# Token rows kept in order, expert places kept in a table and gathered, mean queries and keys added on GpSimd, and mean-key tiles of 64x128, in a fused attention and mixture-of-experts kernel

## The chip, the cores and the metric

The kernel runs on one core of a Trainium2 chip. The core has five engines, each with its own queue of instructions: TensorE (PE in the rows; its weight loads are listed apart as PEld), VectorE (DVE), ScalarE (ACT), GpSimd (POOL) and SyncE (SP). Transfers run on 16 DMA engines; they are started by SP or by POOL here. The metric is the device time of one execution in microseconds (us); lower is better.

## The reference, cut to what matters

Eight batches of eight heads, 576 positions, head dimension 64. Each head has two attentions: one over the means of four neighbouring positions (144 mean queries against 144 mean keys and values, repeated four times), and one over the seven nearest positions. Their sum, laid out as 4608 tokens of 512 numbers, goes to a top-1 mixture of eight experts.

```python
q_d = q.reshape(B, H, Sd, factor, D).mean(axis=3)      # k_d and v_d likewise; factor = 4, Sd = 144
out_up = np.repeat(sm_attn(q_d, k_d, v_d), factor, axis=2)
mask = np.abs(pos[:, None] - pos[None, :]) < factor
out_local = softmax(where(mask, scale * q @ k.T, -1e9)) @ v
x = (out_up + out_local).transpose(0, 2, 1, 3).reshape(B * S, H * D)
e_idx = np.argmax(x @ w_gate, axis=1)
gate_w = softmax(x @ w_gate)[arange(N), e_idx]
eom = sigmoid(x @ w_output_gate)
for e in range(E):                                     # E = 8
    mask = e_idx == e
    out[mask] = gate_w[mask] * eom[mask, e] * (relu(x[mask] @ w1[e]) @ w2[e])
```

## The kernel before, in words

The work is 32 units, each a pair of heads of one batch; four units make a batch. Three functions put a unit's steps into a plan, and `gate` adds the steps of a batch. `Plan.order` is a list scheduler: each step has an engine, a cost, its inputs and the buffers that it uses, and a priority of ten times its slot plus a number from the table `AT`. It puts the steps of all engines into one order, which then stands fixed in every engine's queue. An engine runs its queue strictly in order, so a step that waits holds up all that stand behind it.

`prep(u)` transposes q and k into `T` (PSUM, two buffers; L382) and, by 16 more matmuls for each of q and k with a quarter of an identity as moving operand (L389, `idq`), adds up the means of four beside the transposes. VectorE copies the transposes out (`qT`, `kT`, L397), ScalarE the means (`qd` L402, `kd` L411). VD takes the mean values (L425), ScalarE copies them into `vd` (L431).

`scores(u)` makes the scores of the mean keys (L447, named DS) and of the band (L460, L470), both into the one buffer `S`, and their exponentials into `e` (L452, L476).

`values(u)` makes mean-key values and denominators (V1, L493: 16 products in 64x64 tiles, four of the array's quarters at a time), band denominators (V2, L503) and band values (V3, L515) into the single buffers `PD` and `PL`; then logarithm, exponential of the negative, products (L523 to L549), and on GpSimd the sum of both attentions `xT` (L556) and its f16 copy `x16` (L559).

`gate(b)` makes the logits (L591, L600), picks the expert, ranks the tokens within their expert (L623 to L629, `cum` carries the counts), turns x16 into token rows `xh` of 516 f16 (512 numbers, coefficient, token number; L670, L674), and scatters each row to its place `pos` in the DRAM table `hx_xs`, which has a region for each expert: six indirect transfers a batch on GpSimd (L679). The first 640 rows of each region are filled beforehand with a row whose token number lies out of range (`prefill`, eight transfers on SP).

After the plan, each expert loads its 640 rows with one transfer on SP (L784), transposes them (L750, L751), and runs up (L759, L762, L764) and down (L769, L771); GpSimd scatters the rows to the output by the token number in the row (L772). An expert with more than 640 tokens would go through a loop behind an `If`. The weights of three experts are loaded during attention (`weights`, L693 and L694, two transfers on GpSimd, with a cast to f16), the others when one of three buffers comes free.

Of the kernel before, what the change touches and what calls it, by code (L numbers as in the profile page):

```python
# [8 lines left out]
F32 = mybir.dt.float32  # L9
# [9 lines left out]
SD = 144  # L19
# [47 lines left out]
class Plan:  # L67
# [3 lines left out]
    NEAR = 0.2  # L71
# [85 lines left out]
def kernel(  # L157
# [19 lines left out]
    XW = Dm + 4  # L177
    REG = N
    scale = 1.0 / (D ** 0.5)

    xs_dram = nc.dram_tensor("hx_xs", (E * REG, XW // 2), I32, kind="Internal")

    cst = ctx.enter_context(tc.tile_pool(name="cst", bufs=1))
    wpool = ctx.enter_context(tc.tile_pool(name="wpool", bufs=3))

# [28 lines left out]
    idq = cst.tile([HB, HB + 16], F16)  # L214
# [4 lines left out]
    on_d = cst.tile([128, 3, 64], F32)  # L219
# [9 lines left out]
    zt = cst.tile([128, XW // 2], I32)  # L229
    kd_s = [cst.tile([128, 3, 128], F16, tag=f"kd{i}", name=f"kd{i}") for i in range(3)]  # L230
# [7 lines left out]
    r_vd = ring(sbA, [128, 3, D], F32, "vd", 2)  # L238
# [9 lines left out]
    r_PD = ring(psA, [128, 2, 512], F32, "PD", 1)  # L248
    r_kd = fixed_ring(kd_s)
# [6 lines left out]
    def c_idq():  # L256
        nc.vector.memset(idq, 0.0)
        nc.vector.tensor_scalar_mul(idq[:, 0:HB], id16[0:HB, 0:HB], 0.25)
        for t in kd_s:
            nc.vector.memset(t, 0.0)  # L260
    t_idq = add("c1", 0, "DVE", 1.0, c_idq, deps=[t_id])
# [30 lines left out]
    def c_pv():  # L292
        nc.vector.memset(pv, 0.0)
        nc.vector.memset(on_l, 1.0)
        nc.vector.memset(on_d, 0.0)
        for g in range(NB):
            n = GI[g + 1] - GI[g]
            if g in (0, 1, 4):
                for h in range(2):
                    r0 = 64 * h + 32 * (g % 2)  # L300
                    on = on_d[r0:r0 + n, g // 2:(g // 2 + 2 if g < 4 else 3), :]
                    nc.vector.memset(on, 1.0)
# [538 lines left out]
```

## Time and profile before

| | us |
|---|---|
| median of 3 runs | 519.19 (516.39 to 520.56) |
| profiled execution, time | 523.01 |
| its span, first to last instruction | 520.9 |
| TensorE busy | 419.6 (81%), 7849 matmuls and as many weight loads |
| VectorE, ScalarE, GpSimd busy | 187.4, 199.2, 177.2 |
[...]

TensorE is the only engine that is busy for more than two fifths of the span. The program has two long stages, attention with the gate (up to about 326 us) and the experts (342.6 to 510.5 us), with different limits; shares over the whole span mix them. TensorE's matmuls are pipelined and overlap, so group times add up to more than the time in which the engine was busy.

### The profile page before, as it was taken

How to read it: one execution, taken by the hardware profiler on the slowest of the kernel's cores; microseconds unless marked ns; L12 is line 12 of the kernel's file. 1: busy time of each engine (PE TensorE's matmuls, PEld its weight loads, DVE VectorE, ACT ScalarE, POOL GpSimd, SP SyncE). 2: the span in 40 equal slices, each digit the busy share in tenths (PEclk: the TensorE clock that was granted, in tenths of full speed). 3: DMA queues.
4: the chain of work that ended last, by engine and by line, in shares of the span. 5: the costliest groups of instructions: out<-in, count | busy, mean ns of one | idle time of the engine just before them, and what ended most of it. 6: DMA issues, size and time to landing. Idle time of an engine off the chain costs nothing.

```text
span 520.9 us, 17550 instructions
## 1 busy us (share of the span) xinstructions
PE 419.6 (81%) x7849; PEld 304.6 (58%) x7849; DVE 187.4 (36%) x496; ACT 199.2 (38%) x449; POOL 177.2 (34%) x211
## 2 busy tenths in 40 slices
PE   3787878978897977987997966089959989999991
PEld 2666757656776765765776754065536646566550
DVE  5232443443463462443463453132213313223220
ACT  2243734553563552433463542023313332333331
POOL 6021522535434534424324453405221340512312
PEclk9986986997787895678697886579989997999997
DMA  8998799382992489272212010227893988873202
GB/s 130 178 194 210 172 213 170 75 124 65 173 170 72 80 135 200 53 119 58 60 43 55 18 34 16 78 69 167 133 259 79 202 165 176 198 158 123 91 24 76
DMA packets 85269, 62.74 MB, mean 120 GB/s; under 512 B 49597, under 2 KB 77245, under 8 KB 85184
## 3 DMA queue, kind: packets, MB, share of 16 engines
q0 software_dynamic: 30624, 40.43, 40.6%
q1 hardware_dynamic: 54560, 21.10, 17.9%
q8 instruction: 63, 1.03, 0.8%
q14 instruction: 22, 0.18, 0.1%
HBM read 68.23 MB, written 20.53 MB: 170 GB/s over the span
## 4 chain that ended last, share of the span: by engine, by line
PE 48%; issue 31%; POOL 8%; DMA 4%; ACT 3%; DVE 2%; another core or an unknown queue 2%; POOLq 1%; SPq 0%; DVEq 0%
PE T L389 9%; PE PD L493 7%; POOL out_dram L772 7%; PE T L382 5%; PE PL L515 5%; PE T L425 4%; PE PD L503 4%; PE T L591 3%; PE T L670 3%; DMA qk<-in_k_dram 2%; PE pu L759 2%; PE S L460 2%; PE S L447 2%; PE py L769 1%
## 5 line engine op out<-in xcount | busy, mean ns | idle before, releaser
L759 PE MATMUL pu<-xgT,w 128*128 128x320 f16 x512 | 75.1, 310 | 1.8 <-DVE xgT L751 1.2
L556 POOL TENSOR_TENSOR xT<-xl,xd 128x576 f32<-128x576 f32 x32 | 38.8, 1212 | 102.1 <-DVE xl L549 101.9
L769 PE MATMUL py<-w,hs 128*128 128x512 f16 x320 | 70.4, 379 | 0.0
L679 POOL DMA_INDIRECT hx_xs<-xh,g_pos x48 | 45.1, 939 | 70.1 <-DVE g_pos L660 24.8
L389 PE MATMUL T<-idq,qk 72*64 72x88 f16 (+1 forms) x1024 | 63.0, 312 | 6.3 <-issue 5.9
L759 PEld LDWEIGHTS <-w 128*128 128x128 f16 x512 | 51.8, 101 | 24.5 <-issue 2.9
L772 POOL DMA_INDIRECT out_dram<-y,xg x40 | 39.2, 979 | 64.0 <-ACT y L771 60.2
L762 ACT ACTIVATE hs<-pu 128x320 f16<-128x320 f32 x64 | 28.0, 437 | 83.3 <-PE pu L759 77.7
L389 PEld LDWEIGHTS <-qk 72*64 72x64 f16 x1024 | 47.5, 166 | 9.2 <-issue 9.2
L769 PEld LDWEIGHTS <-hs 128*128 128x128 f16 x320 | 31.3, 98 | 36.4
L764 DVE TENSOR_SCALAR hs<-pu 128x320 f16<-128x320 f32 x64 | 31.4, 491 | 45.7 <-PE pu L759 37.2
L382 PE MATMUL T<-id,qk 72*64 72x72 f16 x1024 | 35.4, 221 | 14.5 <-DMA qk<-in_q_dram 8.9
L493 PE MATMUL PD<-e,vd 64*64 64x72 f32 (+1 forms) x512 | 42.3, 317 | 5.7 <-issue 3.1
L771 ACT ACTIVATE y<-py,xg 128x512 f32<-128x512 f32 x40 | 27.5, 687 | 47.9 <-PE py L769 47.9
L397 DVE COPY kT<-T 128x576 f16<-128x576 f16 x32 | 24.2, 757 | 56.2 <-ACT kd L411 26.5
L493 PE MATMUL PD<-e,on_d 64*64 64x72 f32 (+1 forms) x512 | 42.2, 318 | 2.6 <-issue 2.6
L751 DVE COPY xgT<-tp 128x1024 f16<-128x1024 f16 (+1 forms) x24 | 13.2, 596 | 84.1 <-PE py L769 42.9
L523 ACT ACTIVATE r<-PD 128x582 f32<-128x582 f32 x32 | 21.0, 656 | 57.5 <-PE PD L503 41.6
L397 DVE COPY qT<-T 128x576 f16<-128x576 f16 x32 | 24.2, 757 | 50.9 <-PE T L389 39.2
L493 PEld LDWEIGHTS PD<-e,vd 64*64 64x64 f32 x512 | 36.2, 173 | 9.4 <-issue 8.6
L382 PEld LDWEIGHTS <-qk 72*64 72x64 f16 x1024 | 28.0, 130 | 23.4 <-issue 9.1
L515 PE MATMUL PL<-e,v 64*64 64x57 f32 (+1 forms) x1280 | 33.1, 252 | 10.0 <-issue 9.1
(109 smaller groups left out, 605.8 us busy)
## 6 DMA issues: line engine op xcount, KB each, us to landing
w<-in_moe_w_dram POOLq DMA_DIRECT2D x16, 1024.0 KB
v<-in_v_dram SPq DMA_DIRECT2D x128, 80.0 KB, 4.8
hx_xs<-zt SPq DMA_DIRECT2D x8, 645.0 KB, 5.8
xg<-hx_xs SPq DMA_DIRECT2D x8, 645.0 KB, 4.2
qk<-in_q_dram POOLq DMA_DIRECT2D x7, 576.0 KB
qk<-in_k_dram POOLq DMA_DIRECT2D x7, 576.0 KB
hx_xs<-xh,g_pos POOLq DMA_INDIRECT x48
out_dram<-y,xg POOLq DMA_INDIRECT x40
```

Of the source, the lines that this page charges most:

```text
L382: nc.tensor.transpose(t16[64 * h:64 * h + 64, HB * c:HB * c + HB], src.tile[:, 2 * hp + h, D * c:D * c + D], id16[0:HB, 0:HB])
L389: nc.tensor.matmul(_ap(o, [o.ap[0], [2, w]]), lhsT=src.tile[:, 2 * hp + h, D * (4 * a + m):D * (4 * a + m) + D], rhs=idq[:, 0:w], start=(a ...
L397: nc.vector.tensor_copy(xT.tile.rearrange("p (n c) -> p n c", c=8), T.tile.bitcast(F16)[:, 0:S].rearrange("p (c n) -> p n c", c=8))
L493: nc.tensor.matmul(p[o:o + 64, h, WC + q0:WC + q0 + c1 - c0], lhsT=w[r, blk, :], rhs=et[r, i, WC + c0:WC + c1], start=(blk == 0), stop=(bl ...
L515: nc.tensor.matmul(p[64 * h:64 * h + 64, par, c0:c1], lhsT=vbuf.tile[r, g, h, :], rhs=et[r, h, c0:c1], start=(g == 0), stop=True, skip_gro ...
L556: nc.gpsimd.tensor_tensor(xT.tile[:, hp, :].rearrange("p (n m) -> p n m", m=4), xl.tile.rearrange("p (n m) -> p n m", m=4), _bc(xd.tile, 4 ...
L679: ins = nc.gpsimd.indirect_dma_start(out=xs_dram.ap(), out_offset=bass.IndirectOffsetOnAxis(ap=pos.tile[:, j:j + 1], axis=0), in_=xh.tile[ ...
L759: nc.tensor.matmul(pu[:, 0:c1 - c0], lhsT=w1sb[:, c, 128 * f:128 * f + 128], rhs=xgT[:, c, c0:c1], start=(c == 0), stop=(c == 3))
L762: nc.scalar.activation(hs[:, f, c0:c1], pu[:, 0:c1 - c0], AF.Relu)
L764: nc.vector.tensor_scalar_max(hs[:, f, c0:c1], pu[:, 0:c1 - c0], 0.0)
L769: nc.tensor.matmul(py, lhsT=hs[:, f, 128 * j:128 * j + 128], rhs=w2sb[:, f, :], start=(f == 0), stop=(f == NG - 1))
L772: ins = nc.gpsimd.indirect_dma_start(out=out_rows, out_offset=bass.IndirectOffsetOnAxis(ap=xgi[:, j, Dm // 2 + 1:Dm // 2 + 2], axis=0), in ...
```

## The change

There are five parts.

- **Means.** L389's matmuls go. After VectorE has copied `qT` and `kT`, GpSimd adds neighbours twice (L410 then L413 for q; L410 then two adds of 64 partitions at L418 for k), into `qd` and `kd`. They are sums, so the exponential's scale is divided by 16.
- **Mean-key scores** in four matmuls of 128x128 instead of eight of 128x64. `kd` holds both heads in a block-diagonal form either way.
- **Mean-key values and denominators** in six matmuls with 64x128 tiles instead of sixteen with 64x64. `vd` has columns of ones on both sides of the values, so that one matmul makes both.
- **Token rows.** `xh` (514 f16 now) is written in token order by one plain transfer of SP a batch; two of its three copies out of PSUM go to ScalarE. The prefill goes. The place of each token is turned into one-hot rows (`hi`, `lo`), six matmuls (INV) turn them into a table of 128 lanes x 40 columns, `acc`, that holds the token of each place, and at the end `acc` gives the index lists `gidx` and `sidx`.
- **Experts.** GpSimd gathers the rows of an expert by `gidx` with five indirect transfers (L774), two experts ahead and with three buffers; the next expert's transposes stand between the steps of down; the weights of expert e+3 are asked for behind the five scatters of expert e.

The numbers of `AT`, some of the scheduler's costs and NEAR change as well.

```diff
-    "v": -31.38, "Tq": -3.33, "Tk": 1.99, "evq": -4.73, "evk": 4.65, "qd": -21.49, "kd": -8.83, "VD": 15.17,
+    "v": -55.23, "Tq": -9.85, "Tk": 9.68, "evq": -2.54, "evk": -2.5, "qd": 33.27, "kd": -12.34, "VD": 10.97,
...
-                w = HB + 16 * i
-                for a in range(2):
-                    for m in range(4):
-                        for h in range(2):
-                            o = t32[64 * h:64 * h + 64, 2 * SD + a:2 * SD + a + 1]
-                            nc.tensor.matmul(_ap(o, [o.ap[0], [2, w]]),
-                                             lhsT=src.tile[:, 2 * hp + h, D * (4 * a + m):D * (4 * a + m) + D],
-                                             rhs=idq[:, 0:w], start=(a == 0 and m == 0), stop=(m == 3),
-                                             skip_group_check=True)
...
+            def fn(xT=xT, s2=s2, sd=sd, i=i):
+                pairs = xT.tile.rearrange("p (n m) -> p n m", m=2)
+                nc.gpsimd.tensor_tensor(s2.tile[:, 0:S // 2], pairs[:, :, 0], pairs[:, :, 1], op=ALU.add)
+                if i == 0:
+                    pairs = s2.tile.rearrange("p (n m) -> p n m", m=2)
+                    nc.gpsimd.tensor_tensor(sd.tile, pairs[:, :, 0], pairs[:, :, 1], op=ALU.add)
+                else:
+                    for h in range(2):
...
+                        nc.gpsimd.tensor_tensor(o.rearrange("p b (s x) -> p b s x", s=2),
...
+            e2 = add("kd" if i else "qd", n, "POOL", 1.4 if i else 0.9, fn, deps=[ev, t_ks], uses=[xT, s2, sd])
...
+                nc.tensor.matmul(s[:, i, WC + c0:WC + c1], lhsT=kd.tile[:, blk, :], rhs=qd.tile[:, q0:q0 + c1 - c0],
+                                 start=(blk < 2), stop=True, skip_group_check=True)
...
+                    o, x = p[:, h, WC:WC + SD], et[r, blk % 2, WC:WC + SD]
+                    if blk == 2:
+                        o, x = o.rearrange("p (i n) -> p i n", i=2), et[r, :, WC + SD:WC + DC]
+                    nc.tensor.matmul(o, lhsT=vd.tile[r, blk, D - D * h:3 * D - D * h], rhs=x, start=(blk == 0),
+                                     stop=(blk == 2), skip_group_check=True)
...
+        def fn():
+            for j in range(NJ):
+                nc.tensor.matmul(G.tile[:, 0:NC], lhsT=olo.tile[:, j, :], rhs=hit.tile[:, j, :], start=(j == 0),
+                                 stop=(j == NJ - 1), skip_group_check=True)
+        t10 = add("INV", n, "PE", 0.36, fn, deps=[t8, t9], uses=[olo, hit, G], mode=128, lat=0.16)
...
-        for j in range(NJ):
-            def fn(j=j):
-                ins = nc.gpsimd.indirect_dma_start(
-                    out=xs_dram.ap(), out_offset=bass.IndirectOffsetOnAxis(ap=pos.tile[:, j:j + 1], axis=0),
-                    in_=xh.tile[:, j, :].bitcast(I32), in_offset=None, bounds_check=E * REG - 1, oob_is_err=False)
...
+            nc.sync.dma_start(xs_dram.ap()[S * b:S * b + S, :].rearrange("(j p) d -> p j d", p=P),
+                              xh.tile.bitcast(I32))
+        add("put", n, "SP", 0.8, fn, deps=[t6] + rows, uses=[xh], lat=2.5)
...
-    for r in range(E):
-        add("pre", 2 * r + 1, "SP", 0.8, lambda r=r: prefill(r), deps=[t_cg])
...
+        for e in range(E):
+            w1sb, w2sb = wts[e]
+            xgT, hs, y = xts[e]
+            if e + 2 < E:
+                fetch(e + 2)
+            up(xgT, hs, CAPJ, w1sb)
+            if e + 1 < E:
+                xts[e + 1] = tiles(CAPJ)
+            for j in range(CAPJ):
+                col = CAPJ * (E - 1 - e) + j
+                down(xgs[e], hs, y, j, w2sb, sidx[:, col:col + 1], True)
+                if e + 1 < E and 2 * j < CAPJ:
+                    turn(xgs[e + 1], xts[e + 1][0], CAPJ, 2 * j)
+            if e + 3 < E:
+                weights(e + 3)
```

In TensorE's queue, V1 and V2 of one unit in the middle of attention stand like this before: L389 is the last of the k means, L493 V1, L503 V2, L425 VD and L515 V3.

```order
L389 MATMUL T<-idq,qk_679 64x88
L493 MATMUL PD<-e,vd 64x144 x2
L493 MATMUL PD<-e,on_d 64x144 x2
L493 MATMUL PD<-e,vd 64x72 x2
L493 MATMUL PD<-e,on_d 64x72 x2
L503 MATMUL PD<-e,on_l 64x291 x4
L425 MATMUL T<-v,pv 32x64 x12
L515 MATMUL PL<-e,v 64x60 x4
```

In the changed kernel the same steps are L503 (V1), L512 (V2), L524 (V3), L433 (VD) and L455 (mean-key scores), and L396 is the last transpose of a k.

```order
L396 MATMUL T<-id_70,qk_416 64x72
L524 MATMUL PL<-e,v 64x60 x4
L524 MATMUL PL<-e,v 64x57 x12
L433 MATMUL T<-v,pv 32x64 x12
L503 MATMUL PD<-e,vd_95 128x144 x6
L512 MATMUL PD<-e,on_l 64x291 x4
L455 MATMUL S<-qd,kd_98 128x144
L455 MATMUL S<-qd,kd_98 128x72
```

The means are gone from between transposes and values, V1 is one row of six, and over the whole queue the mean-key scores of a unit stand behind the transposes of the unit after it.

In GpSimd's queue of before, in the middle of attention, the sums and copies of the tokens (L556, L559) stand between the scatters (L679) and the loads of q and k (L345).

```order
L556 TENSOR_TENSOR xT<-xl,xd 128x576
L559 CAST x_1550<-xT 128x576
L679 DMA hx_xs<-xh_90,g_pos 36864x258 x4
L556 TENSOR_TENSOR xT<-xl,xd 128x576
L559 CAST x_1550<-xT 128x576
L679 DMA hx_xs<-xh_90,g_pos 36864x258 x2
L345 DMA qk_2356<-in_q_dram 72x8x512
```

In the changed kernel the same place has the adds for q (L410, L413) and k (L410, L418) of later units between the token sums (L565) and copies (L568).

```order
L410 TENSOR_TENSOR ks_99<-kT 128x288
L418 TENSOR_TENSOR kd_98<-ks_99 64x3x64 x2
L410 TENSOR_TENSOR qs<-qT 128x288
L413 TENSOR_TENSOR qd<-qs 128x144
L565 TENSOR_TENSOR xT<-xl,xd 128x576
L410 TENSOR_TENSOR ks_100<-kT 128x288
L418 TENSOR_TENSOR kd_96<-ks_100 64x3x64 x2
L568 CAST x_4713<-xT 128x576
```

The scatters have left the queue, and five adds a unit have come in, in one line with the steps that wait for VectorE's products.

In the expert stage GpSimd's queue has scatters of the output (L772) and weight loads (L693, L694) before.

```order
L693 DMA w_7638<-in_moe_w_dram 128x4x1024
L772 DMA out_dram<-y,xg 4608x512 x4
L694 DMA w_7639<-in_moe_w_dram 128x8x512
L772 DMA out_dram<-y,xg 4608x512
L693 DMA w_7834<-in_moe_w_dram 128x4x1024
```

In the changed kernel the gathers (L774) come first for three experts, and then once an expert, behind the scatters (L807) and the weights (L726, L727).

```order
L774 DMA xg<-hx_xs,gidx 128x257 x15
L807 DMA out_dram<-y,sidx 4608x512 x5
L726 DMA w_5957<-in_moe_w_dram 128x4x1024
L727 DMA w_5958<-in_moe_w_dram 128x8x512
L774 DMA xg<-hx_xs,gidx 128x257 x5
```

The row loads have moved from SP's queue, where nothing stands behind them but each other, to GpSimd's, behind two weight transfers.

## Rows read from the trace of the kernel before

**Rows 1.** Windows: stages; engine busy (instructions), granted clock, DMA share, GB/s.

```profile
26.20:307.60 281.40, 235.83 (x6415) 188.84 (x6412) 125.20 (x336) 135.00 (x324) 106.48 (x116) 0.81 0.59 114
...
342.60:510.50 167.90, 155.37 (x972) 92.99 (x971) 43.29 (x86) 54.77 (x103) 46.71 (x49) 0.95 0.64 141
```

**Rows 2.** Groups of TensorE from 26.2 to 307.6 us (first and last of 16).

```profile
L389 PE MATMUL T<-idq,qk 72*64 72x72 f16 (+1 forms) x928 | 55.4, 303 | 6.3 <-issue 5.9
...
L629 PE MATMUL T<-cum,ones 96*96 96x48 f16 x7 | 1.5, 210 | 0.0
```

**Rows 3.** Waits of TensorE in the same window: first and eleventh of its reasons.

```profile
PE T L425 <- issue: 11.9, 18, 2.4
...
PE T L591 <- issue: 0.6, 2, 0.4
```

**Rows 4.** Timeline, last unit of attention.

```profile
309.95 0.92 POOL L679 DMA_INDIRECT hx_xs<-xh,g_pos  x1 [0.30 <-issue]
...
311.81 0.35 PE L515 MATMUL PL<-e,v 64*64 64x57 f32 x5 [1.01 <-issue]
...
314.68 0.68 PE L515 MATMUL PL<-e,v 64*64 64x57 f32 x11 [0.47 <-issue]
314.71 0.66 ACT L523 ACTIVATE r<-PD 128x582 f32<-128x582 f32 x1 [9.14 <-remote]
```

**Rows 5.** Windows: the 12 spells of scatters before the last, summed up.

```profile
sum 55.20, PE 36.67 PEld 22.65 DVE 18.00 ACT 9.28 POOL 46.71; mean PE 3.06 PEld 1.89 DVE 1.50 ACT 0.77 POOL 3.89
```

**Rows 6.** Windows of 3 us around one spell of scatters.

```profile
162.00:165.00 3.00, 1.44 (x26) 0.82 (x27) 0.00 (x0) 0.66 (x1) 2.67 (x3) 0.80 0.32 92
165.00:168.00 3.00, 3.00 (x91) 2.72 (x85) 1.06 (x3) 2.07 (x6) 0.70 (x2) 0.50 0.03 5
...
174.00:177.00 3.00, 3.00 (x123) 2.66 (x117) 1.21 (x2) 2.04 (x4) 0.26 (x1) 0.99 0.14 33
```

**Rows 7.** Timeline: V1 and what follows, at full and at half clock.

```profile
301.95 0.34 PE L493 MATMUL PD<-e,vd 64*64 64x144 f32 x2
302.75 0.67 PE L503 MATMUL PD<-e,on_l 64*64 64x291 f32 x8
...
287.90 0.51 PE L493 MATMUL PD<-e,vd 64*64 64x144 f32 x2
289.39 1.02 PE L503 MATMUL PD<-e,on_l 64*64 64x291 f32 x8
290.24 0.75 PE L515 MATMUL PL<-e,v 64*64 64x60 f32 x40
290.92 0.65 PE L670 MATMUL T<-id,x 128*96 128x128 f16 x8
```

**Rows 8.** Groups of GpSimd from 26.2 to 307.6 us.

```profile
L556 POOL TENSOR_TENSOR xT<-xl,xd 128x576 f32<-128x576 f32 x30 | 36.3, 1211 | 98.8 <-DVE xl L549 98.6
L679 POOL DMA_INDIRECT hx_xs<-xh,g_pos x38 | 35.9, 944 | 61.3 <-DVE g_pos L660 24.8 <-DVE xh L674 19.1 <-DMA v<-in_v_dram 8.6
```

**Rows 9.** Chain of waits: start, us, what.

```profile
332.73 2.37 DMA hx_xs<-xh,g_pos
335.69 4.18 DMA xg<-hx_xs
```

**Rows 10.** Timeline, expert stage.

```profile
352.34 8.80 PE L769 MATMUL py<-w,hs 128*128 128x512 f16 x40
...
360.97 1.06 PE L750 MATMUL tp<-id,xg 128*128 128x128 f16 x16
...
362.37 0.38 PE L750 MATMUL tp<-id,xg 128*128 128x128 f16 x4 [0.34 <-DVE xgT L751]
...
362.96 8.85 PE L759 MATMUL pu<-xgT,w 128*128 128x320 f16 x64 [0.21 <-issue]
...
371.65 3.62 PE L769 MATMUL py<-w,hs 128*128 128x512 f16 x16
...
386.62 2.40 PE L750 MATMUL tp<-id,xg 128*128 128x128 f16 x20 [6.17 <-DMA xg<-hx_xs]
```

More of the change, by code (lines that the diff above doesn't have):

```diff
@@ new lines, with count, gather @@
+    more = cst.tile([128, E], I32)
+    most = cst.tile([128, 1], I32)
+    def count():
+        nc.vector.tensor_scalar(more, cntf, scalar1=127.0 - 128.0 * CAPJ, scalar2=0.0, op0=ALU.add, op1=ALU.max)
+        nc.vector.tensor_scalar(more, more, scalar1=7, scalar2=None, op0=ALU.arith_shift_right)
+        nc.vector.tensor_reduce(most, more, axis=AX.X, op=ALU.max)
+    def gather(xg, nj, idx, c0):
+        for j in range(nj):
+            nc.gpsimd.indirect_dma_start(
+                out=xg[:, j, :], out_offset=None, in_=xs_dram.ap(),
+                in_offset=bass.IndirectOffsetOnAxis(ap=idx[:, c0 + j:c0 + j + 1], axis=0),
+                bounds_check=N - 1, oob_is_err=False)
@@ L755, in experts, with turn, up @@
+    def turn(xg, xgT, nj, j0):
+        w = min(2, nj - j0)
+        tp = psF.tile([128, 2, 4, 128], F16, tag="T", name="T", bufs=2)
+        x16 = xg.bitcast(F16)
+        for j in range(w):
+            for c in range(4):
+                nc.tensor.transpose(tp[:, j, c, :], x16[:, j0 + j, 128 * c:128 * c + 128], id16)
+        nc.vector.tensor_copy(xgT.rearrange("p c (j n) -> p j c n", n=128)[:, j0:j0 + w], tp[:, 0:w])
+    def up(xgT, hs, nj, w1sb):
         for f in range(NG):
[L756 to L757 removed]
+            for i in range(2):
+                c0, c1 = 64 * nj * i, 64 * nj * (i + 1)
+                pu = psF.tile([128, 512], F32, tag="U", name="U", bufs=4)
@@ L779, with down @@
-    for e in range(E):
-        if e not in wts:
-            weights(e)
-        base = (E - 1 - e) * REG
-        xg = sbF.tile([128, CAPJ, XW // 2], I32, tag="xg")
-        nc.sync.dma_start(xg, xs_dram.ap()[base:base + 128 * CAPJ, :].rearrange("(j p) d -> p j d", p=128))
-        experts(xg, CAPJ, *wts[e], True)
+    def down(xg, hs, y, j, w2sb, idx, group):
+        py = psF.tile([128, Dm], F32, tag="Y", name="Y", bufs=2)
+        for f in range(NG):
+            nc.tensor.matmul(py, lhsT=hs[:, f, 128 * j:128 * j + 128], rhs=w2sb[:, f, :],
+                             start=(f == 0), stop=(f == NG - 1))
+        nc.scalar.activation(y[:, j, :], py, AF.Copy, scale=xg[:, j, Dm // 2:XW // 2].bitcast(F32))
+        ins = nc.gpsimd.indirect_dma_start(
+            out=out, out_offset=bass.IndirectOffsetOnAxis(ap=idx, axis=0),
+            in_=y[:, j, :], in_offset=None, bounds_check=N - 1, oob_is_err=False)
+        if group:
+            tc.declare_no_dep(ins.ins, group="out_scatter", reason="the rows differ")
+            tc.add_to_no_dep_group("out_scatter", ins.ins)
@@ new lines, in tiles, with fetch @@
+    def tiles(nj):
+        return (sbF.tile([128, 4, 128 * nj], F16, tag="xgT", name="xgT"),
+                sbF.tile([128, NG, 128 * nj], F16, tag="hs", name="hs"),
+                sbF.tile([128, nj, Dm], F32, tag="y", name="y"))
+    with tc.manual_schedule():
+        xgs, xts = {}, {}
+        def fetch(e):
+            xgs[e] = gpool.tile([128, CAPJ, XW // 2], I32, tag="xg", name="xg")
+            gather(xgs[e], CAPJ, gidx, CAPJ * (E - 1 - e))
+        fetch(0)
+        fetch(1)
+        count()
+        xts[0] = tiles(CAPJ)
+        for j0 in range(0, CAPJ, 2):
+            turn(xgs[0], xts[0][0], CAPJ, j0)
+        for e in range(E):
[13 more added lines that the diff above has]
+                weights(e + 3)
@@ L792 @@
         posi = cst.tile([128, 1], I32)
+        ids = cst.tile([128, 1], I32)
+        tok = cst.tile([TB, 1], I32)
+        for b in range(B):
+            for j in range(NJ):
+                nc.vector.tensor_scalar(tok, tok_i[0:TB, j:j + 1], scalar1=float(S * b), scalar2=None, op0=ALU.add)
+                nc.vector.tensor_scalar(posi[0:TB], posall[:, b, j:j + 1], scalar1=float(-REG), scalar2=None, op0=ALU.add)
+                nc.gpsimd.indirect_dma_start(
+                    out=id_dram.ap(), out_offset=bass.IndirectOffsetOnAxis(ap=posi[0:TB], axis=0),
+                    in_=tok, in_offset=None, bounds_check=E * REG - 1, oob_is_err=False)
         for e in range(E):
```

214 lines of the change are left out of this document (100 added, 114 removed), and 12 rows, old and new, of the table AT.

## The prediction

> **What bounds the kernel now.** I read the page's shares first and then left them: TensorE is busy for 81% of the span, but attention and the experts have different limits. So the next view was windows by stage [rows 1]. From the first V1 (26.2 us) to the last (307.6) lie 31 units in 281.4 us, 9.08 us a unit. TensorE is busy for 235.8 of them, 7.61 a unit; VectorE 4.04, ScalarE 4.35, GpSimd 3.43. TensorE sets the pace, with 45.6 us of idle time, 1.47 a unit. Its groups show what it does [rows 2], its waits what stops it [rows 3]: ten of the 14 reasons read "issue", in all 38.7 us, from the first with 11.9 down to 0.2. Real waits for another engine come to under 4 us.
>
> Where the issue stalls fall is to be seen in the timeline [rows 4]: while GpSimd issues scatters one after another, TensorE gets five matmuls, then nothing for a microsecond, and ScalarE sits for 9.14 us. The 12 spells of scatters in the 281 us, taken together [rows 5], hold 55.2 - 36.7 = 18.5 us of TensorE's idle time, 41% of it in 20% of the time. [...]
>
> In the experts (167.9 us for eight, 21.0 each) TensorE is busy for 155.4. Up takes 8.69 us from its start to the start of down, down 8.63, the transposes 1.06 + 0.38 [rows 10]; together 18.8. The rest is waits for rows like the 6.17 us there, a slow clock behind them, and copies between transposes and up.
>
> **The sum is made against the profiled execution**, 523.0 us; its span is 520.9. The median of the runs, 519.2, is 0.7% lower, and I scale by that at the end.
>
> **Means off TensorE.** The 16 groups of [rows 2], L389 first and L629 last, add up to 284.5 us with V1's two simultaneous halves counted once; TensorE was busy for 235.8, so a group's us count 0.83. L389's 55.4 are then 45.9, 1.48 a unit. The end above is 1.79 (no overlap); below I take 1.1. It lies on the path, since TensorE is what the others wait for.
>
> **V1 and the mean-key scores.** 32 matmuls in the trace become 12 and 8 become 4, but columns stay: before, four quarters ran at once over 144 + 144 + 72 + 72 columns, now two halves run over three times 144. So V1, 0.80 us at full clock and 1.49 at half [rows 7], need not shrink: between nothing and a quarter of it, 0.3 a unit; I take 0.1 for both steps, since at half clock it takes 1.86 times as long, as work does that follows the columns. V1 now has another tile shape than V2 behind it. Between V2 and V3, of one shape, starts overlap the end before by 0.17 us, between V3 and a transpose of another shape by 0.07 [rows 7]: 0.1 a change, one or two more a unit. [...] The table's six matmuls a batch (INV), at some 0.2 us start to end, cost 0.08 a unit at most. Busy per unit: 7.61 - 1.48 - 0.1 + 0.1 + 0.1 = 6.2; I use 6.1.
>
> **Scatters out of attention.** The 0.60 us a unit of idle time in the spells goes; one transfer of SP takes the place of six issues on GpSimd and stands on SP only before loads of v that have some units to spare. The issue stalls left, 1.25 - 0.60, shrink with the instructions, of which TensorE fetches a quarter fewer in this stage (1024 + 640 + 128 matmuls go of some 6860, with their loads): 0.49. The 0.22 of other waits stay. Idle: 0.71, pace 6.8. The clock, 0.81 of full now, should gain: five of the spells are followed by such a stretch at half clock, nine us worth about 3.7 each, 0.6 a unit; half of it, 0.3, I take back, since other idle time may pull it down as well. For new waits I add 0.2. **Pace 6.7**, 31 x 2.38 = 74 us saved.
>
> **What the adds cost GpSimd.** 3.43 us a unit less the scatters' 35.9 / 31 leaves 2.27 [rows 1, 8]. The only two-input add of the trace makes 576 elements in 1211 ns, 2.1 ns each. The new ones make 288 + 144 and 288 + 192 + 192 elements: 2.3 us by elements; at the price of the whole row for each of the five, 6.1. So GpSimd has 4.6 to 8.3 us a unit. I take the lower end and some, 5.0, since the adds are half or a third of the row's size; then it is below the pace. They also read f16 with a step of two, which no row shows. [...] The delay itself is covered: mean-key scores stand behind the transposes of the next unit, a slack of about one unit, 6.7 us, against VectorE's copy and at most 3.3 us of adds. If that cover fails, TensorE waits, and V1, V2 and V3 with it.
>
> VectorE loses two of three row copies and gains the one-hots, a few tenths a unit; ScalarE loses the copies of means, gains those two. Both stay below 4.6. The prologue has more constants on VectorE ahead of its first copy, but waits for q and k as before; nothing, plus or minus 3 us.
>
> **The hand-over** from the last V1 to the first up (35 us). V3 of the last unit, 5.3 us among the scatters, needs about 1.3 without them: 4. Then, before, six scatters at 1.22 from 326.6, their landing by 335.1 and the load by 339.9 [rows 4, 9]: 13.3. Now some 3 us of table (VectorE, six matmuls, VectorE), five gathers at 1.22, 2.4 to land: 11.5, with transposes beside the gathers: 3 less with that. Saved: 7, between 2 and 10.
>
> **The experts.** 8 x 18.8 less the first transposes is 148.7, plus 1.0 for a first up at half clock: 149.7 instead of 167.9. The transposes inside down hide their copies; row loads no longer wait for scatters. Saved: 18.
>
> **Sum:** 74 + 7 + 18 = 99; 523 - 99 = 424, scaled to the median 421.
>
> **The rivals.** *GpSimd sets the pace* (0.12): at the price of the full row 8.3 us a unit, saving 24 instead of 74: 470. For it: the queue is strict, adds stand behind token sums that wait for VectorE (98.6 us now [rows 8]). Against it: the two-input add's price should go with its size.
>
> *Half clock* (0.12): with less work TensorE idles more between short steps, and the clock stays at 0.50. V1 takes 1.49 us there against 0.80 [rows 7]; over all steps I take 1.7. The clock of 0.81 means 38% of the time at half, so 6.1 is 5.1 at full and 8.7 at half clock; with 0.3 idle 9.0, no gain in pace: 519 - 2 - 7 - 18 = 492. Against it: the low stretches follow the spells that go.
>
> *Late rows in the experts* (0.10): gathers stand behind two weight transfers, and DMA is at 0.64 over the stage already [rows 1]. Five experts late by some 4 us: 441. For it the waits of before; against it, each gather has about 1.4 experts' time.
>
> *Slower* (0.03): the adds again, but dearer than any row, by their steps of two. From 1.5 us an add GpSimd needs 9.9 a unit, which eats all the rest; at 1.8 the time is 519 + 31 x 2.2 - 25 = 562. That the change does not do what it says is no case: the queues show it.
>
> **How the numbers follow.** The forecast has 0.63. At full clock throughout and 0.9 idle the pace is 6.0, and 519 - 95 - 25 gives 399; I go to 396. Upward the range takes in late rows (441) and most of GpSimd's pace up to 8.2, 468. Half clock, the end of the GpSimd case and slower, some 0.2, lie outside. A measurement of this kernel can tell about 1% from no change. Faster by more than that: 0.95; slower: 0.03; within: 0.02.
>
> **What would show it.** First V1 to last V1 in 200 to 215 us; TensorE busy 6.1 a unit there; no stalls of a microsecond every five matmuls; adds of 0.6, 0.3 and 0.4 us; clock over 0.85 in attention; 18.8 us an expert without waits for xg. The prediction is wrong if the mean-key scores wait for GpSimd in most units, or if the issue stalls stay although the scatters are gone.

## The result, and the profile after

The changed kernel takes 440.16 us (median, 438.84 to 442.69) against 519.88 us (one execution more than in the table of the kernel before): a ratio of 0.847, 95% interval 0.840 to 0.853. Each ratio in this document is taken over the undisturbed executions of both kernels alone, so it need not be that of the medians. The profiled execution took 438.8 us with a span of 437.0 and a mean granted TensorE clock of 0.902; that of the kernel before had 0.851. Its page, with the busy times, the granted clock by slices and the chain of waits by engine:

```profile
PE 347.9 (80%) x6105; PEld 244.9 (56%) x6105; DVE 222.0 (51%) x550; ACT 180.7 (41%) x369; POOL 261.4 (60%) x363
...
PEclk9998997686977889989999855889999999999996
...
PE 39%; DVE 16%; POOL 16%; issue 12%; DMA 8%; ACT 5%; POOLq 1%; DVEq 0%; ACTq 0%
```

In the page of the kernel before, the chain was this:

```profile
PE 48%; issue 31%; POOL 8%; DMA 4%; ACT 3%; DVE 2%; another core or an unknown queue 2%; POOLq 1%; SPq 0%; DVEq 0%
```

"Issue" has fallen from 31% to 12% of the chain, VectorE and GpSimd have come up to 16% each. That fall is not TensorE's stalls in the main: of the 160 us of issue in the chain before, 114 lie in the experts, where the chain runs along GpSimd's scatters. TensorE's own waits are shown below. The windows by stage (attention from the first V1 to the last; the hand-over; the experts) answer to [rows 1]:

```profile
23.10:244.60 221.50, 178.44 (x4845) 140.33 (x4842) 152.88 (x359) 119.30 (x253) 154.17 (x229) 0.89 0.68 123
244.60:271.10 26.50, 12.55 (x145) 9.01 (x146) 12.01 (x44) 4.61 (x9) 10.87 (x11) 0.59 0.25 69
271.10:426.60 155.50, 151.19 (x974) 90.78 (x972) 44.36 (x86) 54.70 (x104) 81.22 (x82) 0.97 0.65 155
```

A unit takes 221.5 / 31 = 7.15 us instead of 9.08: busy 5.76, idle 1.39. Of the 83.9 us that the span lost, 59.9 are here, 8.5 in the hand-over (35.0 to 26.5), 12.4 from the first up to the end and 3.1 ahead of the first V1. TensorE's waits in attention (us in total, times, longest) are of another kind than [rows 3]:

```profile
PE S L468 <- ACT e L460: 9.5, 5, 2.2
PE S L455 <- POOL kd L418: 5.7, 10, 1.0
PE T L706 <- DVE qT L402: 5.4, 6, 1.2
PE PD L503 <- DVE xd L547: 4.3, 5, 1.2
PE T L433 <- issue: 3.2, 2, 2.4
```

Summed over all rows of that view, issue has gone from 38.7 to 10.0 us, and waits for the other three engines from 6.2 (with the last V1's own) to 32.2. In the expert stage nothing waits for rows, and a whole expert takes 18.4 us, except the first: its up starts at 271.1 and down only at 288.0, 16.9 us where each later expert takes 8.7 and the sum had 9.7 for the first, in pieces as in [rows 4]:

```profile
275.60 3.23 PE L794 MATMUL U<-xgT,w 128*128 128x320 f16 x19
280.25 0.70 PE L794 MATMUL U<-xgT,w 128*128 128x320 f16 x4 [1.43 <-issue]
282.32 0.70 PE L794 MATMUL U<-xgT,w 128*128 128x320 f16 x4 [1.37 <-ACT hs L797]
```

Beside it GpSimd issues the ten gathers of the next two experts, one every 1.30 us.

### The profile page after: what moved, and what is told of

Same layout as the page of the kernel before. It is cut to its first block, busy times and chain, and to the rows that moved or that the text cites. A ratio compares the mean times of both kernels' runs of the same rounds, so it can differ in the third digit from the quotient of the medians.

```text
span 437.0 us, 14182 instructions
## 1 busy us (share of the span) xinstructions
PE 347.9 (80%) x6105; PEld 244.9 (56%) x6105; DVE 222.0 (51%) x550; ACT 180.7 (41%) x369; POOL 261.4 (60%) x363
## 4 chain that ended last, share of the span: by engine, by line
PE 39%; DVE 16%; POOL 16%; issue 12%; DMA 8%; ACT 5%; POOLq 1%; DVEq 0%; ACTq 0%
PE U L794 12%; PE Y L804 10%; PE PD L503 4%; POOL xT L565 3%; DMA w<-in_moe_w_dram 3%; DMA qk<-in_k_dram 3%; PE PD L512 3%; POOL out_dram L807 3%; DVE kT L402 2%; DVE xl L554 2%; PE T L706 2%; POOL kd L418 2%; DVE xd L547 2%; ACT r L540 2%; DVE g_og L644 2%
## 5 line engine op out<-in xcount | busy, mean ns | idle before, releaser
L807 POOL DMA_INDIRECT out_dram<-y,sidx x40 | 39.7, 993 | 64.8 <-ACT y L806 35.0
L794 PE MATMUL U<-xgT,w 128*128 128x320 f16 x512 | 75.5, 310 | 3.6 <-issue 1.4
L804 PE MATMUL Y<-w,hs 128*128 128x512 f16 x320 | 73.8, 379 | 0.0
L799 DVE TENSOR_SCALAR hs<-U 128x320 f16<-128x320 f32 x64 | 31.4, 492 | 68.5 <-PE U L794 57.2
L565 POOL TENSOR_TENSOR xT<-xl,xd 128x576 f32<-128x576 f32 x32 | 38.7, 1210 | 24.8 <-DVE xl L558 24.2
L774 POOL DMA_INDIRECT xg<-hx_xs,gidx x40 | 40.7, 1018 | 21.3 <-issue 11.3
L797 ACT ACTIVATE hs<-U 128x320 f16<-128x320 f32 x64 | 27.9, 437 | 59.2 <-PE U L794 58.0
L806 ACT ACTIVATE y<-Y,xg 128x512 f32<-128x512 f32 x40 | 27.5, 688 | 55.7 <-PE Y L804 38.0
L804 PEld LDWEIGHTS <-hs 128*128 128x128 f16 x320 | 30.5, 98 | 31.5
L503 PE MATMUL PD<-e,vd 64*128 64x144 f32 x384 | 40.6, 352 | 5.3 <-DVE xd L547 4.3
L396 PE MATMUL T<-id,qk 72*64 72x72 f16 x1024 | 28.8, 214 | 19.3 <-DMA qk<-in_q_dram 14.0
L410 POOL TENSOR_TENSOR ks<-kT 128x288 f32<-128x288 f16 x32 | 21.9, 685 | 28.9 <-DVE kT L402 28.7
L396 PEld LDWEIGHTS <-qk 72*64 72x64 f16 x1024 | 23.8, 124 | 26.6 <-DMA qk<-in_q_dram 14.2
L503 PEld LDWEIGHTS PD<-e,vd 64*128 64x128 f32 x384 | 32.7, 230 | 7.8 <-issue 2.8
L418 POOL TENSOR_TENSOR kd<-ks 64x192 f16<-64x192 f32 x64 | 32.3, 505 | 4.4
L402 DVE COPY kT<-T 128x576 f16<-128x576 f16 x32 | 24.1, 754 | 17.4 <-PE T L396 17.2
L524 PE MATMUL PL<-e,v 64*64 64x57 f32 (+1 forms) x1280 | 28.6, 232 | 1.1 <-issue 0.9
```

The costliest lines, as they stand in the source:

```text
L396: nc.tensor.transpose(t16[64 * h:64 * h + 64, HB * c:HB * c + HB], src.tile[:, 2 * hp + h, D * c:D * c + D], id16[0:HB, 0:HB])
L402: nc.vector.tensor_copy(xT.tile.rearrange("p (n c) -> p n c", c=8), T.tile.bitcast(F16)[:, 0:S].rearrange("p (c n) -> p n c", c=8))
L418: nc.gpsimd.tensor_tensor(o.rearrange("p b (s x) -> p b s x", s=2), _ap(t, [t.ap[0], [114, 3], [58, 2], [2, 32]]), _ap(t, [t.ap[0], [114, ...
L503: nc.tensor.matmul(o, lhsT=vd.tile[r, blk, D - D * h:3 * D - D * h], rhs=x, start=(blk == 0), stop=(blk == 2), skip_group_check=True)
L524: nc.tensor.matmul(p[64 * h:64 * h + 64, par, c0:c1], lhsT=vbuf.tile[r, g, h, :], rhs=et[r, h, c0:c1], start=(g == 0), stop=True, skip_gro ...
L565: nc.gpsimd.tensor_tensor(xT.tile[:, hp, :].rearrange("p (n m) -> p n m", m=4), xl.tile.rearrange("p (n m) -> p n m", m=4), _bc(xd.tile, 4 ...
```

## The experiments

Three groups of four kernels ran, each group on one chip; the chips were different ones, and that became the main finding. On a chip of the "slow kind" the kernel before takes about 520 us, on one of the "fast kind" about 489. "V1 stretch" is the time from the start of the first product of V1 to the start of the last; by it the two profiles so far have 283.0 and 222.2 us, where the windows above have 281.4 and 221.5.

Two things limit what one run can tell. The list scheduler goes by a step's engine, cost and tile shape, so every edit but that of the gathers can change the order in the queues as well, and a run shows the edit together with its order. And the same attention does not come out the same in every profile: that of the changed kernel has a V1 stretch of 222.2 and 225.8 us on the slow kind, and of 225.7 and 229.4 us on the fast kind (the last in the first run below).

### First group: parts taken back or moved

**Gathers later.**

```
-            if e + 2 < E:
-                fetch(e + 2)
             up(xgT, hs, CAPJ, w1sb)
...
+            if e + 2 < E:
+                fetch(e + 2)
```

> The changed kernel with the gathers of expert e+2 issued behind the down products of expert e instead of ahead of its up products. Theory S (indirect transfers that GpSimd issues back to back keep the other engines short of instructions): of the 10 gathers that run from 268.5 to 281.2 us beside the first up only the first five stay, to about 275, so the first up, 16.9 us in the changed kernel's profile against 9.7 us in the later experts, falls to about 12.3, and the time from 440.2 to about 435.6 (433.5 to 437.5). Rival C (the first up is slow because it is the first: clock just back from 0.59, code or weights cold): the first up stays at 16 to 17 us and the time at 439 to 442.

435.67 us (434.15 to 439.72), and the first up took 11.3 us. That looked like theory S, and it was not: the third group shows the same first up in 10.9 us on another chip with the gathers where they were, and the next two runs of the changed kernel on this very chip, which also leave the gathers in place, have it in 11.0 and 10.6 us. On the slow kind the edit was not run.

**One plain transfer in the kernel before.**

```
-        for j in range(NJ):
-            def fn(j=j):
-                ins = nc.gpsimd.indirect_dma_start(
-                    out=xs_dram.ap(), out_offset=bass.IndirectOffsetOnAxis(ap=pos.tile[:, j:j + 1], axis=0),
...
+        def fn():
+            nc.sync.dma_start(xs_dram.ap()[REG * b:REG * b + S, :].rearrange("(j p) d -> p j d", p=P),
+                              xh.tile.bitcast(I32))
```

> The kernel before with one change: a batch's rows go out in one plain transfer on the SP queue to that batch's own region, not in six scatters on GpSimd, so the placing of rows by expert is left out (each expert takes one batch's tokens; the amount of work stays). Theory S (the scatter spells starve TensorE and ScalarE of instructions and bring half clock behind them): the 18.5 us that TensorE idles in the twelve spells go, waits on issue fall from 38.7 to about 20 us, the clock of the attention rises from .81, and the last spell leaves the hand-over: 519.9 falls to 485 to 500. Rival W (in the spells TensorE waits for work that is late anyway): the idle time moves elsewhere, 508 to 520.

484.23 us (475.98 to 486.74). But on this chip the kernel before took 488.31 (481.7 to 496.8), not 519.9. The waits on issue in attention are 37.9 us; the kernel before has no profile from this chip to set beside them, 38.7 us on the prediction's chip and 34.9 on the third group's. Theory S fails on this chip: without a scatter in attention the issue waits are nowhere near 20 us, and the median is less than 1% shorter. The time lies near S's range only because the chip is faster with the same kernel, and it remained to be seen why.

**Means back on TensorE.** The changed kernel with L389's products, `idq` and the ScalarE copies of the kernel before in place of the five adds.

```
-                nc.gpsimd.tensor_tensor(s2.tile[:, 0:S // 2], pairs[:, :, 0], pairs[:, :, 1], op=ALU.add)
...
+                            nc.tensor.matmul(_ap(o, [o.ap[0], [2, w]]),
+                                             lhsT=src.tile[:, 2 * hp + h, D * (4 * a + m):D * (4 * a + m) + D],
+                                             rhs=idq[:, 0:w], start=(a == 0 and m == 0), stop=(m == 3),
+                                             skip_group_check=True)
...
```

> The changed kernel with the q and k means back as TensorE products with ScalarE copies, all else as changed. Theory P (taking the 1.73 us a unit of mean products off TensorE gave the pace, and what TensorE now waits for on VectorE and GpSimd is only in part cover that would return): busy 5.8 goes to 7.5 us a unit, idle falls from 1.39 to 0.5 to 0.9, pace 8.0 to 8.4 us, so 440.2 + 31 x (0.9 to 1.3) = 467 to 480. Rival R (the rows and gathers did nearly all, and the means are merely moved from one wait to another): idle falls to below 0.2 and the time is 440 to 455. Rival T (both in full, idle stays): pace 8.9, 494.

470.2 us (465.46 to 475.13), a time as theory P has it; the profiled execution is the longest of the four, 475.13. The window of its attention:

```profile
26.10:286.70 260.60, 221.95 (x5781) 175.51 (x5781) 143.66 (x363) 146.53 (x341) 71.40 (x78) 0.88 0.57 105
```

8.41 us a unit, 222 us busy. The same attention without the means has 229.4 and 188.5 on this chip (the run with later gathers) and 225.7 and 186.2 on the third group's: the means are worth 31 to 35 us of attention, 1.0 to 1.13 a unit, all of it busy time. The idle time did not fall as P had it: 1.25 us a unit instead of 0.5 to 0.9. The waits on issue are 13.5 us with 1024 products more (10.2 without them on this chip), so the means were not what filled them.

**Mean adds on VectorE.**

```
-                nc.gpsimd.tensor_tensor(s2.tile[:, 0:S // 2], pairs[:, :, 0], pairs[:, :, 1], op=ALU.add)
+                nc.vector.tensor_tensor(s2.tile[:, 0:S // 2], pairs[:, :, 0], pairs[:, :, 1], op=ALU.add)
...
```

The other calls of the step change in the same way.

> The changed kernel with the five adds of q and k means a unit on VectorE instead of GpSimd. GpSimd falls from 5.0 to about 2.2 us a unit, VectorE gets some 1.4 us and loses up to 0.5 us of stretched small operations. [...] Rival V (VectorE is the next engine, 4.93 us a unit busy: at 5.8 it is as long as TensorE and its queue sets the waits): pace 7.2 to 7.6, 441 to 455.

460.67 us (459.08 to 464.88), beyond rival V's range. Its attention, its longest wait and two of the adds' groups:

```profile
31.30:273.20 241.90, 190.40 (x4706) 147.97 (x4701) 205.48 (x500) 119.22 (x249) 72.24 (x77) 0.82 0.59 108
```

```profile
PE S L455 <- DVE kd L418: 17.5, 18, 2.1
```

```profile
L418 DVE TENSOR_TENSOR kd<-ks 64x192 f16<-64x192 f32 x64 | 24.3, 379 | 1.5
L410 DVE TENSOR_TENSOR ks<-kT 128x288 f32<-128x288 f16 x32 | 17.9, 561 | 1.1
```

An add that takes 505 ns on GpSimd takes 379 here, one of 685 takes 561: 2.30 us a unit instead of my estimate of 1.4. VectorE is busy for 85% of attention, and TensorE's waits for it go to 41.8 us. Against the run with later gathers on the same chip, 9.3 us of the loss fall ahead of the first V1 (31.3 against 22.0 us) and 12.5 in the V1 stretch (241.9 against 229.4). In these orders GpSimd is the better place, although slower.

### Second group: both kernels again, and two parts

**The kernel before, unchanged.**

> The kernel before, unchanged, profiled beside the others of this group, since on the chip of the first experiments it took 488 us at a clock of .89 where the chip of the prediction's profile gave 519.9 at .85. Theory K (the chips differ in the clock they grant in the scatter spells and behind them, not in the work): first V1 to last 250 to 265 us against 283.0, waits on issue about as long as in the first profile (35 to 40 us), and the clock of the attention .87 to .90 against .81. Rival I (the chips differ in how fast instructions arrive): the waits on issue fall to 20 to 28 us and the scatter spells no longer show the low busy share of TensorE (36.7 of 55.2 us).

521.9 us (517.07 to 522.95): this chip is as slow as the prediction's, so neither theory met the chip that it speaks of, and the question had to wait for the third group.

**The changed kernel, unchanged.**

> The changed kernel, unchanged, beside the kernel before on the same chip. Theory K (the gain is partly clock that the first chip withheld from the kernel before): 438 to 444 us whatever the chip, so a ratio of .89 to .91 where the chip runs the kernel before in 488 us, .847 where it takes 520 us. Rival I: the ratio stays at .84 to .86 on any chip, which means 410 to 420 us where the kernel before takes 488.

440.66 us (438.88 to 442.1), ratio 0.853 (0.848 to 0.859); on a chip of the slow kind both theories have that. Attention before and after, on this chip:

```profile
26.70:309.10 282.40, 234.91 (x6462) 189.37 (x6455) 126.58 (x337) 135.11 (x324) 107.52 (x117) 0.82 0.59 113
```

```profile
22.30:248.10 225.80, 182.16 (x4861) 141.92 (x4853) 153.46 (x360) 119.22 (x253) 153.96 (x229) 0.89 0.68 121
```

**Joining add on VectorE.**

```
-            nc.gpsimd.tensor_tensor(xT.tile[:, hp, :].rearrange("p (n m) -> p n m", m=4),
+            nc.vector.tensor_tensor(xT.tile[:, hp, :].rearrange("p (n m) -> p n m", m=4),
```

> The changed kernel with the add that joins local and mean-key values (128 x 576 f32, 1210 ns on GpSimd) on VectorE. [...] Theory V (after the five mean adds went to VectorE the time rose to 460.7: VectorE's queue sets the waits): 444 to 455 us, waits of TensorE for VectorE up by 5 us or more. Rival G (an add of 1.2 us that blocks small VectorE operations for its whole length costs more than the same add in VectorE's own queue): 428 to 437 us, and the gate's six-element operations fall from some 1170 ns to below 400 ns.

436.95 us (431.45 to 442.86); its ratio, 0.840 (0.829 to 0.851), overlaps that of the unmoved one. The V1 stretch is 227.2 us, not shorter. Theory V falls: the time did not rise, and TensorE's waits for VectorE went from 13.4 to 11.3 us. What rival G said of the small operations is right, what it said of the time isn't shown. VectorE's groups in attention, first of the changed kernel, then with the add moved:

```profile
L657 DVE TENSOR_SCALAR g_se<-g_se 96x6 f32<-96x6 f32 x7 | 8.2, 1172 | 0.2
L644 DVE TENSOR_TENSOR g_og<-g_L,g_oh 96x48 f32<-96x48 f32 x7 | 7.3, 1046 | 0.2
...
L694 DVE TENSOR_TENSOR acc<-acc,T 128x40 f32<-128x40 f32 x6 | 1.1, 187 | 0.0
```

```profile
L565 DVE TENSOR_TENSOR xT<-xl,xd 128x576 f32<-128x576 f32 x30 | 24.7, 825 | 0.5
L644 DVE TENSOR_TENSOR g_og<-g_L,g_oh 96x48 f32<-96x48 f32 x7 | 2.8, 400 | 0.2
L657 DVE TENSOR_SCALAR g_se<-g_se 96x6 f32<-96x6 f32 x7 | 2.1, 304 | 0.2
```

The two groups give back 10.6 us of VectorE (8.2 + 7.3 to 2.1 + 2.8), but the add itself brings 24.7.

**Small tiles back.** V1 as twelve products, mean-key scores as eight.

```
-                    nc.tensor.matmul(o, lhsT=vd.tile[r, blk, D - D * h:3 * D - D * h], rhs=x, start=(blk == 0),
-                                     stop=(blk == 2), skip_group_check=True)
+                    for a in range(2):
+                        nc.tensor.matmul(o[D * a:D * a + D], lhsT=vd.tile[r, blk, D + D * (a - h):2 * D + D * (a - h)],
+                                         rhs=x, start=(blk == 0), stop=(blk == 2), skip_group_check=True)
...
-                nc.tensor.matmul(s[:, i, WC + c0:WC + c1], lhsT=kd.tile[:, blk, :], rhs=qd.tile[:, q0:q0 + c1 - c0],
-                                 start=(blk < 2), stop=True, skip_group_check=True)
+                for h in range(2):
+                    nc.tensor.matmul(s[64 * h:64 * h + 64, i, WC + c0:WC + c1], lhsT=kd.tile[:, blk, 64 * h:64 * h + 64],
+                                     rhs=qd.tile[:, q0:q0 + c1 - c0], start=(blk < 2), stop=True, skip_group_check=True)
```

> The changed kernel with V1 as twelve products of 64x64 tiles instead of six of 64x128 a unit, and the mean-key scores as eight products instead of four. Theory N (halves that run side by side cost what one of twice the width costs): the time stays within 3 us of the changed kernel on the same chip, V1's groups show two halves of about 40 us each. Rival I (each product more costs its issue): 320 products more, 5 to 12 us slower.

445.05 us (441.92 to 447.75). That is 4.4 us more than the changed kernel on this chip, a little outside theory N's 3 us and short of rival I's 5 to 12, and the intervals of the two ratios (0.852 to 0.872 here) overlap. The V1 stretch is 224.5 us against 225.8, so no gain of the larger tiles in pace is shown; the first V1 comes at 27.5 us instead of 22.3, because in this order the scores of the second unit and the transposes of one unit more stand ahead of it, with 2.4 us of issue waits among them. The issue waits in the stretch doubled, 13.1 to 26.5 us, while waits for other engines fell from 29.4 to 20.1; how much of that is the tiles and how much the order, this run can't tell. The longest:

```profile
PE PL L526 <- issue: 10.1, 7, 2.9
PE PD L505 <- issue: 9.8, 6, 3.0
```

They are V3 and V1, the steps with many short products side by side.

V1 itself shows a price of the larger tiles. In the changed kernel, at full and at half clock:

```profile
112.74 1.01 PE L503 MATMUL PD<-e,vd 64*128 64x144 f32 x12
113.68 0.72 PE L512 MATMUL PD<-e,on_l 64*64 64x291 f32 x8
...
128.90 1.81 PE L503 MATMUL PD<-e,vd 64*128 64x144 f32 x12
130.64 1.25 PE L512 MATMUL PD<-e,on_l 64*64 64x291 f32 x8
```

From the start of V1 to the start of V2, which has another tile shape, it takes 0.94 and 1.74 us; in the kernel before it took 0.80 and 1.49 [rows 7], and with the small tiles back it is 0.79 and 1.50 again. The columns are the same, so the 0.15 us (0.24 at half clock) go with the change of shape.

### Third group: the other kind of chip, with all four kernels

**The kernel before.**

> The kernel before, unchanged, for a profile on the same chip as the next run. Theory C (what differs between chips is the clock granted around the scatter spells): TensorE waits 37 to 41 us on issue in the attention on any chip; where the time is about 520 its clock in the attention is .81 to .82 and its busy time 235 to 238 us, where the time is about 488 they are .87 to .89 and 208 to 215 us. Rival I (the supply of instructions differs): the waits on issue differ by 15 us or more between a 520 us and a 488 us profile.

489.0 us (480.28 to 495.13), and so a chip as the first group's.

**Plain transfer.**

> The kernel before with one plain transfer a batch in place of six scatters, as in the first group, leaving out the placing of rows by expert, now with a profile of the kernel before from the same chip. Theory C (a scatter spell costs clock, not instructions): the waits on issue stay at 36 to 40 us; where the kernel before takes about 520 us this takes 480 to 495, by a busy time of TensorE that falls from 235 to about 208 us; where it takes 488 this gains only 3 to 8 us. Rival S (my prediction's step: TensorE's idle 18.5 us in the spells go): the waits on issue fall to about 20 us. Rival O (the first group's small gain was all there is): 514 to 518 where the kernel before takes 520.

480.79 us (476.83 to 484.05), ratio 0.981 (0.964 to 0.998). Attention of the kernel before on this chip, then with the plain transfer:

```profile
25.30:276.20 250.90, 211.57 (x6468) 173.29 (x6459) 125.87 (x337) 134.95 (x325) 107.24 (x116) 0.88 0.68 129
```

```profile
26.30:276.20 249.90, 214.73 (x6459) 175.58 (x6452) 130.68 (x337) 135.56 (x324) 71.05 (x78) 0.88 0.67 129
```

On this chip the scatters cost attention 1 us, less than one profile differs from another. The gain is behind it: last V1 to first up 31.5 to 24.8 us, where six scatters stand in the open, and first up to the end 180.3 to 175.8. The waits on issue are 34.9 and 30.4 us.

The first twelve spells of scatters, one of them alone and all summed up, on the second group's chip and on this one (same kernel, same length of a spell):

```profile
126.74:131.48 4.74, 2.90 (x59) 1.68 (x52) 0.83 (x4) 0.66 (x1) 3.82 (x4) 1.00 0.38 101
...
sum 41.35, PE 27.88 PEld 17.52 DVE 16.13 ACT 6.59 POOL 33.99; mean PE 2.32 PEld 1.46 DVE 1.34 ACT 0.55 POOL 2.83
```

```profile
120.66:125.40 4.74, 4.66 (x176) 3.88 (x168) 2.35 (x6) 3.00 (x8) 3.82 (x4) 1.00 0.26 68
...
sum 41.38, PE 39.46 PEld 30.41 DVE 21.80 ACT 20.18 POOL 34.01; mean PE 3.29 PEld 2.53 DVE 1.82 ACT 1.68 POOL 2.83
```

59 products against 176 beside the same four scatters; ScalarE 6.6 against 20.2 us of work. The timelines of that spell, chip by chip:

```profile
129.33 0.92 POOL L679 DMA_INDIRECT hx_xs<-xh,g_pos  x1 [0.30 <-issue]
129.50 0.33 PE L425 MATMUL T<-v,pv 128*32 128x64 f32 x5 [0.40 <-issue]
130.23 0.34 PE L425 MATMUL T<-v,pv 128*32 128x64 f32 x6 [0.40 <-issue]
```

```profile
121.98 0.97 POOL L679 DMA_INDIRECT hx_xs<-xh,g_pos  x1 [0.31 <-issue]
121.99 0.91 PE L425 MATMUL T<-v,pv 128*32 128x64 f32 x24
122.82 0.81 PE L515 MATMUL PL<-e,v 64*64 64x60 f32 x40
```

Theory C has the clock and the busy time right, and of the issue waits one total (40.5 us on the slow chip) but not the others (34.9 on this one, 30.4 with the plain transfer); rival I's difference of 15 us between the chips did not come, it is 5.6, and rival S's 20 us did not come either. But the total hides that the stalls are others: on the slow chip there are 54, of which 25 end within a spell (12.2 us; L425 has 14 of these), on the fast one 27, longer, of which 2 end within a spell (1.4 us). So on the slow chip a spell does bring issue stalls, which theory C denied; why, no trace here shows.

**Changed kernel, unchanged.**

> The changed kernel, unchanged, on the same chip as the run before this one. It issues no scatters in the attention and took 440.2 and 440.7 us on two occasions: 438 to 443 us, whatever the kernel before takes on this chip.

435.19 us (429.69 to 436.84), ratio 0.883 (0.869 to 0.897). That is a little below the expected 438, and far from the 410 to 420 us that rival I of the second group had for a fast chip. On this chip the gathers do not starve TensorE either, and the first up runs through in 10.9 us where the second group's took 16.5 and the first profile's 16.9:

```profile
274.20 11.11 PE L794 MATMUL U<-xgT,w 128*128 128x320 f16 x64
```

Its V1 stretch is 225.7 us.

**Both edits.**

> The changed kernel with both edits that looked good alone: the gathers of expert e+2 behind the downs of expert e, and the join of local and mean-key values on VectorE. If they add, each works in another stage (first up 16.5 to about 11.3 us; waits of TensorE for other engines 29 to about 21 us in the attention, less what VectorE's longer queue takes back): 429 to 434 us, against 439 to 442 for the changed kernel on the same chip. If the second is within the scatter of the runs: 434 to 437.

432.31 us (429.43 to 434.9), ratio 0.885 (0.874 to 0.896), the same as the changed kernel's. First up 10.6 against 10.9, V1 stretch 221.0 against 225.7. No version was shown to be better than the changed kernel; on a chip of the slow kind this one was not tried.

## Why the prediction was right, and where it was not

The prediction, 421 with a range of 396 to 468, holds 440.2; the direction and the place were right. Its forecast for the profiled run was 424, the run took 438.8. The difference by stages: pace 7.15 instead of 6.7, +14; experts 155.5 instead of 149.7, +6; hand-over -1.5; prologue -3.1. Together +15.

That the busy time came out as forecast, 5.76 us a unit where 6.1 less 0.3 for the clock was put, is luck in part: the means gave less than I took, and, by the comparison of the two chips, the scatters took more busy time with them than I put. The signs of being wrong did not show: the mean-key scores waited for GpSimd's `kd` 10 times in 31 units, 5.7 us in all, and the issue stalls went. But the forecast is one for the slow kind of chip: on the fast kind the same change saves 54 us, not 80.

**Means off TensorE: right, too large.** I took 1.48 us a unit; the run with the means back gives 1.0 to 1.13 (31 to 35 us). My factor from a group's us to busy time (0.83) came from a run at a clock of 0.81; at 0.88 L389's group is 49.4, not 55.4.

**Scatters out of attention: right for the chip in hand.** I took 0.60 a unit of idle and 0.3 of clock, 28 us. The 0.3 rests on [rows 6]: between the two last windows there the granted clock stays at 0.50, with TensorE busy all the time:

```profile
168.00:171.00 3.00, 3.00 (x74) 2.69 (x69) 2.19 (x5) 0.95 (x4) 0.09 (x1) 0.50 0.46 104
171.00:174.00 3.00, 3.00 (x80) 2.53 (x73) 0.76 (x1) 1.62 (x4) 1.78 (x2) 0.50 0.05 11
```

Between the two chips, the kernel before differs by 31.5 us in its V1 stretch (282.4, 250.9); its spells hold 13.5 us of idle on one and 1.9 on the other, the busy time is 23 us longer, the clock 0.82 against 0.88. So the total fits, but not its make-up: 0.75 a unit is busy time at a lower clock, and 0.26 is idle. The plain transfer, which costs or saves nothing on the fast kind, was not run on the slow kind, so that all of the 31.5 are the scatters' is argued from the spells, not shown.

On the slow kind attention lost 56.6 us (282.4 to 225.8); on the fast kind 25.2 (250.9 to 225.7), although the means alone are worth 31 to 35. So the rest of the change, with table and copies, costs attention about 10 us (260.6 with the means back; the kernel before has 250.9, with the plain transfer on the same chip 250.6), all of it busy time of TensorE (222.0 against 211.6 and 207.6). INV's products are 2.4 of these, and V1's change of shape about 5 (31 x 0.15, more at half clock); the rest is open. That -35 + 10 - 31.5 gives the slow kind's -56.5 is no check of the parts: two of them are differences from the same profiles, and the sum says only that the changed kernel has the same V1 stretch on both kinds (225.8 and 225.7).

**V1 and scores in larger tiles: nearly.** V1's group is 39.6 us, one half's time before, but V2 starts 0.15 to 0.24 us later behind it, where I had set a gain of 0.1 against a change of shape at 0.1. The issue stalls that I meant to shrink by instruction count, to 0.49 a unit, went to 0.32. With the small tiles back they are 26.5 us, against 13.1 with the large ones and 40.5 before the change on that chip: these tiles, with the order that they bring, go with half of the fall.

**New waits: the term that was too small.** I added 0.2 us a unit; waits for other engines rose by (32.2 - 6.2) / 31 = 0.84. I had set VectorE at "a few tenths" more, below 4.6; it is 4.93, and more than the table's own steps is in that: tiny gate operations stand still while GpSimd adds. A timeline of the changed kernel:

```profile
239.37 1.21 POOL L565 TENSOR_TENSOR xT<-xl,xd 128x576 f32<-128x576 f32 x1 [2.37 <-DVE xl L558]
239.43 1.18 DVE L657 TENSOR_SCALAR g_se<-g_se 96x6 f32<-96x6 f32 x1
240.64 0.16 DVE L658 SCALAR_TENSOR_TENSOR g_den<-g_ez,g_se 96x6 f32<-96x6 f32 x1
```

Six elements a partition take as long as GpSimd's 576 beside them. What these stalls cost in time could not be told apart: with the add moved they shrink, VectorE has the add instead, and the pace stays.

**GpSimd: right.** 4.97 us a unit against 5.0; the adds take 0.68, 0.43 and 0.51 us, 2.8 a unit for 2.3. It does not set the pace: rival 1 falls. Its share in the new waits is 9.2 of 32.2 us.

**Half clock:** fell, 0.89. **Late rows:** fell, no wait for xg. But their price came from elsewhere: the experts' first up ran beside gathers. I had seen what scatters do to TensorE and put ten indirect transfers beside up without asking the same of them. The first up takes 16.5 to 17.4 us in all four profiles of the changed kernel and its variants on the slow kind, and 10.6 to 11.3 in all five on the fast kind, three of these with the gathers in the same place; that on the slow kind the gathers are the reason for these some 6 us is argued from their place in time, as they were not moved there. On the fast kind the time from the first up to the end fell by 20.0 us (180.3 to 160.3), close to the 18 of the sum.

**Hand-over:** 8.5 us for 7. In the rival *Slower* the sum has a slip without weight: 2.27 + 5 x 1.5 is 9.8, not 9.9.

## What to carry to other kernels

When a stall looks like a property of the machine (an engine short of instructions beside another's transfers), profile the unchanged kernel on a second chip before crediting an edit with removing it; the first up that looked repaired in the first experiment was the chip's. Work moved off the bounding engine comes back in part as waits for the engines that took it (26 us of them here, for 57 us less busy time, what went with the scatters included), and the price of each small operation there must be taken with its neighbours running (L657: 1172 ns, and 304 with GpSimd's add gone). And where a scheduler orders the queues, an edit of one step can move many others, so look at the order before crediting the edit.

## What the runs showed of the hardware

Chips differ in what goes on beside indirect transfers issued by GpSimd. On two occasions (521.9 and 519.9 us) TensorE got 59 and 61 products through in one spell of 4.74 us, on one (489.0 us) 176, with the same instructions and the same 0.92 to 1.01 us for each scatter. The changed kernel, which issues no such transfers in attention, is nearly the same on both, 440.7 and 435.2. Why the chips differ is open, and since each chip was used on one occasion, the chip itself and its condition at that time can't be told apart.

An operation of VectorE can be held for the whole length of one on GpSimd: L657 takes 1172 ns in the mean, and 304 with the 1.2 us add gone from GpSimd; L644 takes 1046 and 400. Not every operation is held. Of two adds into `acc` of the same size in the changed kernel, the one that reads PSUM (L694) takes 183 to 196 ns, also beside a GpSimd operation (at 107.43 us, beside L410). The one with both inputs in SBUF (L696) takes 199 to 1099 ns: 1.10 us at 245.70 beside GpSimd's L565, 0.20 at 260.18 with nothing on GpSimd. What decides which operation is held is open: L644 and L696 have both inputs in SBUF, while L657 reads one tile.
